# Regrouping query weights as they land, moving FFN weight loads behind a transpose, and a new front order in a linear-attention block kernel

## Chip, cores and metric

The kernel runs on one core of a Trainium2 chip. The metric is the device time of one execution in microseconds; the median of the runs is compared.

## What is computed

The input x has 2048 tokens of 640 features. Block A is attention with 32 heads of 20 features over four segments of 512 tokens, with a running memory between the segments; block B is a feed-forward block with 1728 hidden features. Both add to the residual. All tensors are bf16.

```python
q, k, v = heads(ln(x) @ wq), heads(ln(x) @ wk), heads(ln(x) @ wv)      # 32 heads, 4 segments of 512
for s in range(4):
    p = softmax(qs @ ks.T * scale + causal_mask)
    a_dot = p @ vs
    a_mem = (phi(qs) @ M) / (phi(qs) @ z + 1e-6)
    outs.append(g * a_mem + (1 - g) * a_dot)
    M, z = M + phi(ks).T @ vs, z + sum(phi(ks))
h = x + concat(outs) @ wo
out = h + silu(ln(h) @ w1) @ w2
```

## The kernel before

The kernel is one straight program for all engines. `build` declares small tasks, each with a name, the engines that may do it, and what it reads and writes. A long string, `ORDER`, gives the sequence of all tasks by hand. Each entry is a task name, then optionally the engine (`/A` ScalarE, `/D` VectorE, `/G` GpSimd, `/S` SyncE) and, after a colon, the slots that its new buffers take (PSUM banks above all). Each engine does its tasks in the order of the list; semaphore waits are derived from reads and writes. A DMA is a task of the engine that issues it, so its place in the list is its place in that engine's queue. The loads of x and of the weights, and all DMA transposes, are issued by SP; the on-chip copies `vt` by SP or ACT. An issuing engine waits at the DMA's place until its inputs are there, and everything behind it on that engine waits too.

The names that matter here, for segment 0 (the first digit) unless said otherwise:

- `x0`, `x1`, `x2`, `x4`, `x8`, `x12`: loads of 128-token blocks (one, one, two, four, four, four). `w_q0`, `w_q1`, `w_q2`: the query weights, chunks 0, 1 to 2 and 3 to 4 of five chunks of 128 rows; `w_k0`, `w_k1` the key weights in two parts. They land raw in `sT` (`wraw`).
- `re_wq0` to `re_wq4`, `re_wk0` to `re_wk4` (the function `rearr`, L692 on ACT, L694 on DVE): a weight's columns regrouped into `wqr` or `wkr`, one task for each of five head groups. Groups 0 to 2 take two operations, groups 3 and 4 three. Each group has 128 columns, four heads of 32 rows: 20 features of one head and 12 (or 8 and 4) borrowed features of a head of the last twelve.
- `n1_st`, `n1_r`, `n1_ap`: statistics, reciprocal root and application of the first layer norm for a token block. `n1_tp` and `n1_te`: transposing by TensorE (L778) and evacuation into `hT` (L790, L791), for blocks 0 to 3. `n1_tr4` and on: the same for the blocks of the next segment by a DMA transpose into `xT` (L798).
- `pr0cwx`, `pr0cwy`: projection of head group c, w = 0 for query and 1 for key, tokens 0 to 255 (x) or 256 to 511 (y) (L866; L871 for `pr010x` and `pr040x`, which work block by block). `qe...`: its evacuation (L882 on ACT, L883 on DVE).
- `vt00` to `vt011` (L914): on-chip copies that collect the borrowed features into three more groups, `QZV`. Those with numbers 0, 3, 6, 9 read groups 0 to 2, the others groups 3 and 4; all of them read the x and the y half.
- `qk0x1`, `qk0x2`, `qk0x3`, `qk4x1`, ... (L964): scores, and `e0x1`, ... their exponentials on ACT (L976), either in two halves (`e0x10`, `e0x12`) or in one (`e0x1+`). `mk...`: the causal mask on GpSimd (L987). The names with 4 use the copied groups. `v00` to `v13` (L827): value projections, and `ve` their evacuation (L842). `av`, `oe`, `tn`, `nm`: probabilities times values and the division. `ex`, `pha`, `phb`, `kt`, `mz`: phi of the keys, its DMA transpose (L1207) and the memory.
- `ot` and `wo` (L1264, L1272): the output's DMA transpose and the output projection. `w_w1_0` to `w_w1_4`: the first FFN weight, one load of 432 KB for each chunk. `h1` (L1307) and `h2` (L1349): the FFN.

The two value projections at the seam of segment 0 and 1 are `v11`, `v12`, `v10`, `v13`, in this order; each reads what `n1_tr5`, `n1_tr6`, `n1_tr4` and `n1_tr7` bring. SP's part of the list in that stretch reads, with the tasks of other engines left out:

```text
vt02 vt011 vt05 vt08 vt04 vt06 vt09 vt01 n1_tr5 kt02 n1_tr6 kt00 w_w1_2 n1_tr4 w_w1_3 w_w1_1 n1_tr7 ot1 ot0 w_w1_4
```

Of the kernel before, what the change touches and what calls it, by code (L numbers as in the profile page):

```python
# [324 lines left out]
D = 640  # L325
# [31 lines left out]
epsg0:0 vpad0 zpad w2z/G:0 fill30:7 warm iota mt mta mtb mm7 x0:0 x1:4 mm0 n1_st1/A:0,0 w_q0:0 w_q1 w_q2 epsc sel  # L357
halfc n1_st0/D:5 n1_r0/G n1_r1/D n1_ap0:0 n1_tp0:4 n1_te0a/A:0 n1_ap1:1 n1_tp1:0 n1_te0b/A n1_te1b/D n1_te1a/A w_k0
re_wq1/D:0 pr010x:4 re_wq4/A re_wq2/D pr020x:2 qe020x/A:0 qe010x/A:0 re_wq3/D re_wq0/D pr000x:5 pr040x:6 w_k1
re_wk2/A:0 qe000x/A:0 re_wk1/D qe040x/A:0 pr011x:0 qe011x/A re_wk0/D pr001x:2 pr021x:5 qe001x/A qe021x/A x2:10,5  # L360
n1_st2/D:3 n1_r2/G qk0x10:0 pr030x:7 w_wv0:0 w_wv1 n1_st3/D:1 n1_r3/G e0x10:4 x4:2,1,11,3 qe030x/A:0 w_wo:0 beta
w_w1_0:0 e0x12 re_wk3/D pr031x:6 n1_ap2:2 re_wk4/D x8/S:6,7,8,9 n1_ap3:0 n1_tp2:0 n1_te2/D n1_st6:4 n1_tp3:4 n1_r6/G
n1_te3/A qe031x/D pr041x:7 qe041x/D qk0x20:0 e0x2+:6 pr030y:4 qe030y/D pr031y:5 qe031y/A pr041y:6 qe041y/A pr040y:7
qe040y/A vt02/S:0 vt011/S vt05/S vt08/S n1_st5:1 qk0x30:0 vt04/S mk0x1_0 mk0x1_256 n1_st4:5 n1_r5/G n1_ap5:1 e0x3+:0
n1_ap6:2 pr000y:4 qe000y/D lsc0 vt07/A pr021y:6 qe021y/D pr001y:5 qe001y/D pr011y:7 ex021:0 qe011y/D pr020y:1 n1_r4/D
mk0x3_0 qe020y/D mk0x3_256 vt010/A pr010y:6 qe010y/D vt00/A vt03/A vt06/S v03:2 ve03/D:0 ex001:1 mk0x3_384 mk0x2_0
v00:4 ve00/D qk0y10:0 e0y12:5 mk0x1_384 pha021:1 pha001:2 v01:6 e0y10 mk0y1_0 mk0x2_256 vt09/S phb021 vt01/S qk4x10:2
phb001 lsc1 n1_st7:7 e4x1+:2 vpad1 v02:0 ve01/D av0x:6 mk4x1_0 n1_ap4:3 n1_r7/G qk4x20:2 e4x2+:1 n1_tr5:0 mk4x1_256
mk4x1_384 ve02/D lsc2 lsc3 oe0x/D:0 mk4x2_0 mk4x2_256 av2x:7 ex041:1 oe2x/D:1 kt02:0 n1_tr6 mk0y1_256 mm2 kt00:1 v11:0
qk4x30:2 e4x30:3 pha011:0 ve11/D:1 tn0x:6 nm0x:3 e4x32 mk4x3_0 pha031:1 qk0ya0:0 mk4x3_256 n1_ap7:2 mk4x3_384 v12:6  # L370
e0ya+:4 w_w1_2 ve12/D av4x:4 oe4x/D:0 mz00:5 ma00/A:2,5 qk1ya0:0 e1ya2:0 tn2x:6 nm2x:0 av6x:7 oe6x/D:1 e1ya0 tn4x:6
nm4x:1 qk2ya0:2 kvz e2ya2:1 tn6x:7 mm3 nm6x:2 n1_tr4 v10:0 n1_st11:2 e2ya0 qk0y20:4 e0y2+:6 w_w1_3 w_w1_1 mk0y2_0
kg00/G:0 mk0y2_256 n1_tr7 v13:2 n1_r11/G qk3ya0:4 e3ya0:3 ve10/D n1_st9:6 n1_r9/D pha041:2 ex031:2 mm6 ve13/D ot1:0
wo1:0 n1_st8:3 e3ya2 ot0 ex011:0 wo0:2 rs1 n2_st1:0 mk0y1_384 w_w1_4 phb011 qk4ya0:4 e4ya0:2 n2_r1/D kg02/G e4ya2 rs0
n2_ap1:0 n2_st0:0 pr101:0 qe101/A:0 av0y:1 qk0y30:2 e0y3+:0 w_w2_0/S pr120:6 zf0 n2_r0/D oe0y/D:0 pr100:7 mk0y3_0
ex101:0 qk5ya0:2 n2_ap0:3 e5ya2:4 n2_tr1:0 phb041 qe100/D e5ya0 qe120/D:0 pr121:0 qe121/D qk4y10:4 mk0y3_256 tn0y:1
# [36 lines left out]
h2_2_2 e19b2 h2_2_3 mk18a_0 n2_r5/G qk19a0:0 h2_3_0:4 h2_3_1 e19a2:0 o2 ad17:0 vp22/S e19a0 n2_ap5:3 n2_tr5 out2/S
mk19a_0 vp24/S ex200:0 kh14/D av18:6 oe18/D:0 vt210/A phb200 qk20b0:0 e20b+:3 h2_3_2 mk19b_0 h2_3_3 o3 vp25/S ex201:1
# [48 lines left out]
def build(nc, es, A_x, A_wq, A_wk, A_wv, A_wo, A_beta, B_x, B_w1, B_w2, out):  # L463
# [209 lines left out]
    def rearr(k, wi, dst, prio):  # L673
# [3 lines left out]
        for c in range(5):  # L677
# [10 lines left out]
            def emit(eng, ops=ops, rr=rr, ww=ww):  # L688
                fns = []
                for o, i_ in ops:  # L690
                    if eng == AC:
                        fns.append(lambda e, o=o, i_=i_: e.activation(out=o, in_=i_, func=ACT.Identity))  # L692
                    else:
                        fns.append(lambda e, o=o, i_=i_: e.tensor_copy(out=o, in_=i_))  # L694
# [730 lines left out]
```

## Time and profile before

| | |
|---|---|
| median of 3 runs | 298.89 us (298.69 to 299.05) |
| profiled execution | 298.33 us |
| its span in the trace | 296.6 us |
| TensorE, ScalarE, VectorE, GpSimd busy | 285.0, 217.5, 222.8, 139.9 us |
| granted TensorE clock | 1.00 |

The span is what the profiler recorded from the first to the last instruction; the device time of the same execution is 1.7 us longer. Busy times are sums of the durations of instructions. Matmuls are pipelined, so a busy TensorE is not one at its peak.

### The profile page before, as it was taken

Reading aid. Unit: us, or ns where it says so; the run is one execution under the profiler, and the core shown is the slowest. Engines: PE = TensorE matmul, PEld = TensorE weight load, DVE = VectorE, ACT = ScalarE, POOL = GpSimd, SP = SyncE. Lnnn points to the kernel's source line nnn. Section 1 sums busy time; section 2 is a strip of 40 time slices with the busy share of each in tenths; the row PEclk is TensorE's granted clock in tenths of the full one; section 3 lists DMA queues with packets and bytes.
Section 4 is the critical chain, followed back from the end, with each engine's and each line's share of the span. In section 5 each row is a group of like instructions: output and inputs, shape, how many; then the busy total and the mean of one; then the engine's idle time right before and its main releaser. Section 6 shows DMA issues by size and latency. Waiting matters only on the chain.

```text
span 296.6 us, 7437 instructions
## 1 busy us (share of the span) xinstructions
PE 285.0 (96%) x2991; PEld 167.6 (56%) x2991; DVE 222.8 (75%) x506; ACT 217.5 (73%) x266; POOL 139.9 (47%) x257
## 2 busy tenths in 40 slices
PE   7897879999999999999999999999999999999997
PEld 5775445545665455566643444465665457764575
DVE  3897889768989789899678967759967688626522
ACT  5875979999999899999879999788759751014400
POOL 6246834744656477646525656355576620200000
PEclk9999999999999999999999999999999999999999
DMA  7968772804943321254462400154181023220002
GB/s 208 366 209 114 192 105 68 221 18 98 168 89 75 74 39 26 37 111 66 97 140 51 77 1 2 26 75 88 20 102 32 0 59 76 68 67 25 22 22 91
DMA packets 49906, 25.40 MB, mean 86 GB/s; under 512 B 39488, under 2 KB 48032, under 8 KB 49872
## 3 DMA queue, kind: packets, MB, share of 16 engines
q1 hardware_dynamic: 48204, 23.18, 37.3%
q10 hardware_dynamic: 1668, 1.74, 1.9%
q8 instruction: 24, 0.39, 0.6%
q14 instruction: 10, 0.08, 0.1%
HBM read 10.41 MB, written 2.62 MB: 44 GB/s over the span
## 4 chain that ended last, share of the span: by engine, by line
PE 76%; DVE 8%; DMA 7%; ACT 4%; POOL 2%; issue 2%; SPq 1%; DVEq 0%; ACTq 0%
PE ps_all L1349 19%; PE ps_all L1307 15%; PE ps_all L866 12%; PE ps_all L1272 7%; PE ps_all L964 7%; PE ps_all L827 5%; PE ps_all L1008 5%; ACT PT L976 3%; DMA x_tok<-in_A_x_dram 3%; DMA xT<-xn_rot 2%; PE ps_all L1038 1%; DMA w_sb<-w_sb 1%; PE ps_all L1092 1%; PE ps_all L1225 1%; POOL PT L987 1%
## 5 line engine op out<-in xcount | busy, mean ns | idle before, releaser
L976 ACT ACTIVATE PT<-ps_all 128x1024 bf16<-128x1024 f32 (+1 forms) x120 | 153.1, 1310 | 17.7 <-PE ps_all L964 16.5
L987 POOL TENSOR_SCALAR_AFFINE_SELECT PT<-PT 128x512 bf16<-128x512 bf16 x128 | 81.5, 647 | 59.1 <-ACT PT L976 57.0
L1349 PE MATMUL ps_all<-w_sb,sT 128*128 128x320 bf16 (+2 forms) x462 | 64.9, 295 | 0.0
L1307 PE MATMUL ps_all<-hT,w_sb 128*128 128x512 bf16 (+1 forms) x325 | 63.0, 337 | 0.5 <-DVE sT L1322 0.4
L1316 ACT ACTIVATE th<-ps_all 128x512 f32<-128x512 f32 (+2 forms) x70 | 34.0, 505 | 35.1 <-PE ps_all L1307 31.0
L1349 PEld LDWEIGHTS ps_all<-w_sb,sT 128*128 128x128 bf16 x462 | 43.2, 98 | 18.3 <-issue 1.8
L1322 DVE SCALAR_TENSOR_TENSOR sT<-th,ps_all 128x512 bf16<-128x512 f32 (+2 forms) x70 | 37.8, 561 | 17.1 <-ACT th L1316 16.1
L1307 PEld LDWEIGHTS ps_all<-hT,w_sb 128*128 128x128 bf16 x325 | 29.8, 98 | 25.9 <-issue 3.2
L763 POOL TENSOR_TENSOR rst<-rst,eps_c 128x1 f32<-128x1 f32 x32 | 18.4, 579 | 25.1 <-DVE rst L757 23.5
L742 DVE BATCH_NORM_STATS2 stt<-x_tok 128x6 f32<-128x320 bf16 x62 | 27.2, 481 | 1.8 <-DMA x_tok<-in_A_x_dram 1.4
L1362 DVE SCALAR_TENSOR_TENSOR x_tok<-ps_all,x_tok 128x640 bf16<-128x640 f32 (+3 forms) x18 | 13.3, 745 | 16.7 <-PE ps_all L1349 16.6
L1070 POOL TENSOR_TENSOR otok<-on 128x320 bf16<-128x320 bf16 x24 | 19.0, 796 | 11.5 <-DVE on L1062 11.5
L1272 PE MATMUL ps_all<-wo_sb,oT 128*128 128x320 bf16 x160 | 23.8, 299 | 0.0
L883 DVE CAST QK<-ps_all 128x512 bf16<-128x512 f32 x23 | 15.7, 688 | 8.8 <-PE ps_all L866 8.7
L1062 DVE TENSOR_TENSOR on<-ps_all,rd 128x640 bf16<-128x640 f32 x24 | 19.8, 825 | 0.9
L827 PE MATMUL ps_all<-wv_sb,xT 128*128 128x320 bf16 x120 | 18.3, 299 | 1.6 <-DMA xT<-xn_rot 1.3
L1272 PEld LDWEIGHTS ps_all<-wo_sb,oT 128*128 128x128 bf16 x160 | 15.0, 98 | 7.2 <-issue 1.8
L866 PE MATMUL ps_all<-xT,wkr 128*128 128x512 bf16 x75 | 18.7, 380 | 0.0
L866 PE MATMUL ps_all<-xT,wqr 128*128 128x512 bf16 x75 | 18.2, 380 | 0.0
L842 DVE CAST Vx<-ps_all 128x640 bf16<-128x640 f32 x15 | 12.3, 819 | 5.9 <-PE ps_all L827 5.8
L1008 PE MATMUL ps_all<-PT,Vx 128*32 128x512 bf16 (+3 forms) x384 | 16.4, 301 | 0.1
L769 DVE TENSOR_SCALAR xn_rot<-x_tok,mvt,rst 128x640 bf16<-128x640 bf16 x32 | 14.8, 473 | 1.7 <-POOL rst L763 1.0
(106 smaller groups left out, 338.3 us busy)
## 6 DMA issues: line engine op xcount, KB each, us to landing
w_sb<-in_B_w_dram SPq DMA_DIRECT2D x5, 432.0 KB, 6.1
x_tok<-in_A_x_dram SPq DMA_DIRECT2D x3, 640.0 KB, 8.4
w_sb<-in_B_w_dram SPq DMA_DIRECT2D x3, 480.0 KB, 4.4
out_dram<-x_tok ACTq DMA_DIRECT2D x8, 160.0 KB, 1.8
out_dram<-x_tok SPq DMA_DIRECT2D x7, 160.0 KB, 2.0
QKV<-QK SPq DMA_DIRECT2D x12, 72.0 KB
wo_sb<-in_A_wo_dram SPq DMA_DIRECT2D x1, 800.0 KB, 10.0
sT<-in_A_wq_dram SPq DMA_DIRECT2D x2, 320.0 KB, 4.3
```

The costliest lines, as they stand in the source:

```text
L742: T.add(DV, lambda e, hh=hh: e.bn_stats(out=stt[:, s, 6 * hh:6 * hh + 6], in_=xb[:, 320 * hh:320 * hh + 320]), reads=R((xa, xsub)), writes ...
L827: fns.append(lambda e, c=c, hh=hh: e.matmul(bank(ps, hh)[:, 0:320], lhsT=xT_[:, c, 128 * i:128 * i + 128], rhs=wv_sb[:, c, 320 * hh:320 * ...
L866: fns = [lambda e, kc=kc: e.matmul(bank(ps)[:, lo:hi], lhsT=wt[:, kc, c, :], rhs=xT_[:, kc, lo:hi], start=(kc == 0), stop=(kc == NC - 1)) ...
L964: fns.append(lambda e, j=j, o=o, r=r, q0=q0, q1=q1, qa=qa, ka=ka: e.matmul(ps_all[:, o:o + q1 - q0], lhsT=ka[32 * r:32 * r + DH, 128 * j:1 ...
L976: T.add(AC, lambda e: e.activation(out=pt[:, pta.slot, q0:q0 + nq, 0:width], in_=sc3[:, b0:b0 + nq, 0:width], func=ACT.Exp, scale=SCALE), ...
L987: T.add(PO, lambda e: e.affine_select(out=v, in_=v, pattern=[[0, 4], [1, 128]], compare_op=ALU.is_ge, fill=0.0, base=0, channel_multiplier ...
L1008: fns.append(lambda e, j=j, r=r, h=h, pa=pa, pt=pt, co=co, q0=q0, ji=ji: e.matmul(bank(po)[32 * r:32 * r + 32, q0:hi], lhsT=Vx[:, vx.slot, ...
L1272: fns.append(lambda e, c=c, hh=hh: e.matmul(bank(ps, hh)[:, 0:320], lhsT=oT[:, c, 128 * i:128 * i + 128], rhs=wo_sb[:, c, 320 * hh:320 * h ...
L1307: fns = [lambda e, c=c: e.matmul(bank(ps)[:, lo:hi], lhsT=w1_sb[:, c, 128 * f:128 * f + 128], rhs=hT[:, c, lo:hi], start=(c == 0), stop=(c ...
L1316: T.add(AC, lambda e: e.activation(out=th[:, tha.slot, lo:hi], in_=bank(ps)[:, lo:hi], func=ACT.Tanh, scale=0.5), reads=R((ps, [0])), writ ...
L1322: T.add(DV, lambda e: e.scalar_tensor_tensor(out=sT[:, f, lo:hi], in0=th[:, tha.slot, lo:hi], scalar=1.0, in1=bank(ps)[:, lo:hi], op0=ALU. ...
L1349: fns.append(lambda e, f=f, t0=t0, fr=fr, hh=hh, n=n: e.matmul(bank(pa, hh)[:, 0:n], lhsT=sT[:, f, t0:t0 + 128], rhs=w2_sb[:, fr, c0 + 320 ...
```

## The change

In `rearr`, the query groups 1 and 2 become two tasks each: `re_wq1` and `re_wq2` regroup chunks 0 to 2 and wait for `w_q0` and `w_q1` only; `re_wq1b` and `re_wq2b` regroup chunks 3 and 4 and wait for `w_q2`. The other groups stay as they were.

```diff
-            rr, ww = [(sT0, ["k0", "k1"] if wi else ["q0", "q1", "q2"])], [(W[k], [c])]
+            ww = [(W[k], [c])]
+            pieces = [("", 0, 3, ["q0", "q1"]), ("b", 3, 5, ["q2"])] if wi == 0 and c in (1, 2) else \
+                [("", 0, 5, ["k0", "k1"] if wi else ["q0", "q1", "q2"])]
...
-                for o, i_ in ops:
+                for o, i_ in [(o[:, k0:k1], i_[:, k0:k1]) for o, i_ in ops]:
...
-            G.task(f"re_{k}{c}", {DV: 0.36 if c < 3 else 0.42, AC: 0.72}, emit, rr, ww, prio + c)
+            for tg, k0, k1, sub in pieces:
+                rr = [(sT0, sub)]
+                G.task(f"re_{k}{c}{tg}", {DV: 0.36 if c < 3 else 0.42, AC: 0.72},
+                       lambda eng, emit=emit, rr=rr, k0=k0, k1=k1: emit(eng, rr=rr, k0=k0, k1=k1), rr, ww, prio + c)
```

The list is redone up to `v02`, and three loads are moved behind that point. The front of the new list:

```text
x0:3 x1:6 mm0 n1_st1/A:0,0 w_q0:0 halfc sel n1_st0/D:3 epsc w_q1 n1_r0/D re_wq2/A:0 w_q2 w_k0 n1_ap0:2 n1_tp0:0
n1_te0a/A:0 n1_r1/D n1_ap1:0 n1_tp1:2 n1_te1a/A re_wq1/D re_wq4/D n1_te0b/A n1_te1b/A re_wq2b/D pr040x:1 qe040x/A:0
w_k1 re_wk0/A:0 x2:0,1 w_wv0:0 re_wq1b/D pr010x:2 qe010x/A:0 re_wq3/D re_wq0/D pr000x:4 re_wk1/D w_wv1 pr011x:6
qe000x/A:0 qe011x/A x4:9,2,10,5 pr001x:5 qe001x/A re_wk2/D pr021x:7 qe021x/A:0 n1_st2/D:1 w_wo:0 n1_st3/D:4 qk0x10:0
e0x10:3 pr030x:4 qe030x/A:0 pr020x:6 qe020x/A e0x12 n1_r2/G n1_ap2:0 n1_tp2:0 re_wk3/D pr031x:4 beta re_wk4/D n1_r3/G
n1_ap3:1 n1_tp3:5 n1_te3/A n1_te2/D pr041x:7 qe041x/D qk0x20:0 e0x22:0 pr041y:6 n1_st4:2 qe031x/D pr030y:5 qe030y/D
x8/S:7,8,4,11 n1_r4/D e0x20 mk0x2_0 pr031y:7 qe041y/D pr040y:2 pr010y:0 qk0x30:3 qe031y/A qe040y/D pr001y:1 mk0x1_0
mk0x2_256 pr020y:2 pr000y:7 mk0x1_256 mk0x1_384 vt07/A:0 vt011/S vt01/S vt02/S vt010/S vt08/A e0x3+:4 vt04/S n1_st5:0
qe010y/D qe001y/D pha001:1 qe000y/D n1_r5/D qe020y/D pr011y:1 qe011y/D n1_ap5:3 pr021y:0 qe021y/A v03:6 mk0x3_0
n1_st7:0 mk0x3_256 mk0x3_384 n1_r7/G pha021:2 vt06/A n1_st6:6 vt09/S qk0y10:2 vt00/S vt05/S ve03/D:0 n1_r6/G v00:0
n1_tr5:0 ex001:0 phb001 kt00:0 vt03/A lsc0 e0y1+:5 mk0y1_0 n1_ap4:1 n1_tr4 ex021:2 n1_ap6:0 n1_tr6 mk0y1_256 ve00/D
phb021 kt02:1 lsc1 vpad1 v01:6 ve01/D w_w1_0:0 qk4x10:2 e4x12:2 e4x10 mk4x1_0 v02:0
```

In the list before, the same stretch is:

```text
x0:0 x1:4 mm0 n1_st1/A:0,0 w_q0:0 w_q1 w_q2 epsc sel halfc n1_st0/D:5 n1_r0/G n1_r1/D n1_ap0:0 n1_tp0:4 n1_te0a/A:0
n1_ap1:1 n1_tp1:0 n1_te0b/A n1_te1b/D n1_te1a/A w_k0 re_wq1/D:0 pr010x:4 re_wq4/A re_wq2/D pr020x:2 qe020x/A:0
qe010x/A:0 re_wq3/D re_wq0/D pr000x:5 pr040x:6 w_k1 re_wk2/A:0 qe000x/A:0 re_wk1/D qe040x/A:0 pr011x:0 qe011x/A
re_wk0/D pr001x:2 pr021x:5 qe001x/A qe021x/A x2:10,5 n1_st2/D:3 n1_r2/G qk0x10:0 pr030x:7 w_wv0:0 w_wv1 n1_st3/D:1
n1_r3/G e0x10:4 x4:2,1,11,3 qe030x/A:0 w_wo:0 beta w_w1_0:0 e0x12 re_wk3/D pr031x:6 n1_ap2:2 re_wk4/D x8/S:6,7,8,9
n1_ap3:0 n1_tp2:0 n1_te2/D n1_st6:4 n1_tp3:4 n1_r6/G n1_te3/A qe031x/D pr041x:7 qe041x/D qk0x20:0 e0x2+:6 pr030y:4
qe030y/D pr031y:5 qe031y/A pr041y:6 qe041y/A pr040y:7 qe040y/A vt02/S:0 vt011/S vt05/S vt08/S n1_st5:1 qk0x30:0 vt04/S
mk0x1_0 mk0x1_256 n1_st4:5 n1_r5/G n1_ap5:1 e0x3+:0 n1_ap6:2 pr000y:4 qe000y/D lsc0 vt07/A pr021y:6 qe021y/D pr001y:5
qe001y/D pr011y:7 ex021:0 qe011y/D pr020y:1 n1_r4/D mk0x3_0 qe020y/D mk0x3_256 vt010/A pr010y:6 qe010y/D vt00/A vt03/A
vt06/S v03:2 ve03/D:0 ex001:1 mk0x3_384 mk0x2_0 v00:4 ve00/D qk0y10:0 e0y12:5 mk0x1_384 pha021:1 pha001:2 v01:6 e0y10
mk0y1_0 mk0x2_256 vt09/S phb021 vt01/S qk4x10:2 phb001 lsc1 n1_st7:7 e4x1+:2 vpad1 v02:0
```

Behind `v02` the sequence of compute tasks is unchanged, except that `n1_ap4` has gone ahead. `n1_tr5`, `kt00`, `n1_tr4`, `n1_tr6`, `kt02` have gone ahead, in this order. `w_w1_1` and `w_w1_3` now follow `n1_tr7`, and `w_w2_0` stands one place earlier. SP's stretch becomes:

```text
vt011 vt01 vt02 vt010 vt04 vt09 vt00 vt05 n1_tr5 kt00 n1_tr4 n1_tr6 kt02 w_w1_0 w_w1_2 n1_tr7 w_w1_1 w_w1_3 ot1 ot0 w_w1_4
```

More of the change, by code (lines that the diff above doesn't have):

```diff
@@ L356 @@
 ORDER = """
[L357 to L376, printed above, removed]
```

183 lines of the change are left out of this document (102 added, 81 removed).

## The prediction

> **What bounds the kernel now.** I read the page first, then busy time by stretch, then the waits of TensorE, then the timelines of PE, ACT and SP around the two largest waits. The first two lines below are of the page (busy time; the chain that ended last), the rest is busy time by stretch: PE, PEld, DVE, ACT, POOL with their counts, then clock, DMA share and GB/s.
>
> ```profile
> PE 285.0 (96%) x2991; PEld 167.6 (56%) x2991; DVE 222.8 (75%) x506; ACT 217.5 (73%) x266; POOL 139.9 (47%) x257
> PE 76%; DVE 8%; DMA 7%; ACT 4%; POOL 2%; issue 2%; SPq 1%; DVEq 0%; ACTq 0%
> 8.30:12.23 3.93, 3.93 (x45) 3.46 (x45) 3.42 (x16) 3.44 (x12) 0.54 (x2) 1.00 1.07 372
> 12.23:21.54 9.31, 9.27 (x108) 7.29 (x108) 8.89 (x31) 8.41 (x12) 3.92 (x10) 1.00 0.79 266
> 21.54:28.20 6.66, 5.11 (x57) 3.33 (x55) 5.15 (x13) 2.57 (x3) 4.93 (x9) 1.00 0.62 107
> 28.20:44.20 16.00, 13.18 (x198) 7.59 (x197) 13.28 (x31) 13.93 (x12) 9.88 (x20) 1.00 0.87 145
> 44.20:60.00 15.80, 15.50 (x199) 8.93 (x196) 13.81 (x34) 15.34 (x18) 9.99 (x19) 1.00 0.58 145
> ```
>
> TensorE is the bound of the whole (285.0 of 296.6 us). The list is changed almost only ahead of 50 us, so what counts is idle TensorE there. From 8.30 to 21.54 there is none (3.93 + 9.27 = 13.20 busy of 13.24). From 21.54 to 28.20 it idles 1.55 us, from 28.20 to 44.20 2.82 us, and in the second of these ACT is busier than PE (13.93 of 16.00). The waits of PE, for 0 to 44 us (three rows) and for 44 us to the end (the last row, its longest): us, times, longest.
>
> ```profile
> PE ps_all L964 <- DMA w_sb<-w_sb: 1.6, 1, 1.6
> PE ps_all L827 <- DMA xT<-xn_rot: 1.3, 1, 1.3
> PE ps_all L964 <- DVE otok L1137: 0.9, 1, 0.9
> PE ps_all L1307 <- DVE sT L1322: 0.4, 1, 0.4
> ```
>
> Three waits are worth a look: scores (L964) for the on-chip copies "vt", the value projection v13 (L827) for the transpose n1_tr7, and scores behind a division on DVE. After 44 us no wait is over 0.4 us, so a shift won there should reach the end one to one.
>
> **The change part by part.** First the clearest: w_w1_1 and w_w1_3 go behind n1_tr7. Timelines of SP, PE and ACT (start, length), and two rows of DMA issues (KB where known, us from issue to landing).
>
> ```profile
> 33.02 1.05 SPq L581 DMA_DIRECT2D w_sb<-in_B_w_dram  x2
> w_sb<-in_B_w_dram SPq DMA_DIRECT2D x2, 432.0 KB, 6.3
> 35.03 1.21 SPq L798 DMA_TRANSPOSE xT<-xn_rot  x1
> xT<-xn_rot SPq DMA_TRANSPOSE x1, 7.4
> 42.45 1.53 PE L827 MATMUL ps_all<-wv_sb,xT 128*128 128x320 bf16 x10 [1.31 <-DMA xT<-xn_rot]
> 43.91 0.40 PE L964 MATMUL ps_all<-w_sb 20*128 20x256 bf16 x8
> 44.24 2.89 PE L1272 MATMUL ps_all<-wo_sb,oT 128*128 128x320 bf16 x20
> 41.18 1.88 ACT L976 ACTIVATE PT<-ps_all 128x2048 bf16<-128x2048 f32 x1 [0.21 <-PE ps_all L964]
> 44.36 1.02 ACT L976 ACTIVATE PT<-ps_all 128x1024 bf16<-128x1024 f32 x1 [1.30 <-PE ps_all L964]
> ```
>
> The two loads go out at 33.02, the transpose at 35.03 lands 7.4 us later (42.4), and v13 stands still for 1.31 us. In the new list w_w1_0 and w_w1_2 precede n1_tr7 instead, but they follow five transposes that end near 31 (below), so they go out about 2 us ahead of the old pair. With the 6.3 us of the old pair they land by 37.7 (the second goes out at 31.4) and n1_tr7, 2.5 us after them as in the trace (42.4 against 33.6 + 6.3 = 39.9), by about 40.2. PE comes to v13 at 42.45 - 1.31 = 41.14. The stall goes. What is late next is ACT: qk3ya0 (43.91) takes PSUM slots 4 to 7, which e0y2+ reads until 41.18 + 1.88 = 43.06. So qk3ya0 starts at about 43.13 and its exponential, 0.45 us behind it as now (43.91 to 44.36), at 43.58: 44.36 - 43.58 = 0.78 us won, not 1.31. Above it is bounded by ACT's whole gap, 1.30; below by 0.
>
> Next, the front. wq groups 1 and 2 are regrouped in chunks 0 to 2 and chunks 3 and 4. Rows: an issue and its landing, ACT and PE timelines, and regrouping copies by shape (busy, mean ns).
>
> ```profile
> 2.21 0.43 SPq L581 DMA_DIRECT2D sT<-in_A_wq_dram  x1
> sT<-in_A_wq_dram SPq DMA_DIRECT2D x1, 320.0 KB, 4.1
> 6.51 0.91 ACT L790 ACTIVATE hT<-ps_all 128x384 bf16<-128x384 f32 x2 [1.11 <-PE ps_all L778]
> 8.30 0.72 PE L871 MATMUL ps_all<-hT,wqr 128*128 128x128 bf16 x10 [0.94 <-DVE wqr L694]
> L694 DVE COPY wqr<-sT 128x400 bf16<-128x400 bf16 x4 | 1.1, 272 | 0.0
> L694 DVE COPY wkr<-sT 128x80 bf16<-128x80 bf16 x2 | 0.4, 190 | 0.0
> L692 ACT ACTIVATE wkr<-sT 128x240 bf16<-128x240 bf16 x1 | 0.4, 404 | 0.0
> ```
>
> The second load (chunks 1 and 2) lands at 2.21 + 4.1 = 6.31, while ACT waits until 6.51 anyway. re_wq2 now runs there first: two operations, of 240 and 144 elements, 404 ns and somewhat less, ending near 6.9, so the first evacuation of hT starts 0.4 us late. ACT then does all four evacuations (one was on DVE), each 0.45 us (0.91 for two) and the last two behind the second transpose: the last ends near 8.6, and the first projection, now pr040x, ends at about 8.9 against 8.85. I take 0.05 us later; the bounds are 0.4 later (the held evacuation in full) and 0.3 earlier (the copies that TensorE waited for until 8.30 are done sooner). On DVE a split group costs four copies where there were two; from 272 ns at 400 elements and 190 at 80 each extra copy is near 0.2 us, so about 0.3 us a group. It costs nothing as long as DVE then waits for the k weights anyway; without that cover it is 0.3 to 0.6 us.
>
> [...]
>
> From 8.30 to 21.54 TensorE does the same 20 half projections, transposes and scores in another order, without a hole to close. So the last projection ends no earlier; 0 won here. In the new list six more evacuations of the y half run on DVE, and layer norm statistics go between them; walking through both engines by the durations above I find no projection waiting for its PSUM slot.
>
> Then the copies vt. Rows: the chain that ended last (start, length), ACT's timeline, and the durations of the copies' issues on ACT (min/median/max in ns).
>
> ```profile
> 21.75 0.44 DVE w_sb L883
> 23.86 3.78 DMA w_sb<-w_sb
> 18.38 1.88 ACT L976 ACTIVATE PT<-ps_all 128x2048 bf16<-128x2048 f32 x1
> 18.49 1.63 ACTq L914 DMA_DIRECT2D w_sb<-w_sb  x1
> 23.99 0.63 ACT L889 ACTIVATE ex<-w_sb 128x512 bf16<-128x512 bf16 x1 [2.64 <-DVE Vx L842]
> 28.22 1.88 ACT L976 ACTIVATE PT<-ps_all 128x2048 bf16<-128x2048 f32 x1 [1.48 <-PE ps_all L964]
> L914 ACTq DMA_DIRECT2D w_sb<-w_sb x4: 701/856/1626, 18.5 to 23.1; - x4
> ```
>
> The last evacuation of the y half ends at 21.75 + 0.44 = 22.19; the copies that read it follow, and the last lands at 23.86 + 3.78 = 27.64, 5.45 us behind it. Only then come qk4x10 and, at 28.22, ACT's long run. In the new list five copies follow the last evacuation as now (three on SP, two on ACT), so the 5.45 us stay. But that evacuation is now qe021y on ACT behind e0x3+, and e0x3+ stands behind vt07 and vt08, which ACT itself issues. Queued behind those two issues on ACT are e0x3+, qe021y, vt06, ex001, vt03 and the exponentials of qk0y10; v03 waits for e0x3+ as well (slot 6), and the copies for qe021y. vt07 can go at about 18.48, when its inputs are ready, as now. With 0.8 us an issue (the median is 0.86) e0x3+ runs from 20.1 to 22.0 and qe021y ends at about 22.3: 0.1 us later than 22.19. The issue of 1.63 us I read as one that had a small activation (lsc0) queued ahead of it behind a 1.88 us exponential; in the new list nothing of that kind precedes vt07. Bounds: 0.05 earlier (0.70 each; then TensorE is later than ACT) and 1.8 later (1.63 each).
>
> The exponentials of qk4x10 come in two halves: 2 x 1.02 less the overlap in place of 1.88, so 0.06 us more. ACT's run from 28.22 to 43.06 is otherwise the same work in the same order, and the third wait of PE (0.9 us) lies inside it, where ACT is the later of the two. w_w1_0 leaving the first flood of loads lets x8 land sooner, which nobody waits for: 0.
>
> Sum: -0.78 + 0.10 + 0.06 = -0.62 us (the 0.05 of the start is contained in the 0.10, since the later of two arrivals counts). The profiled execution took 298.33 us (span 296.6) and lies 0.56 us under the median of the runs, 298.89; I apply the difference to both: 297.7 for a like execution, 298.3 as the median.
>
> **The rivals.** Rows for them: issues on SP, the projection v12, landings.
>
> ```profile
> 27.28 1.29 SPq L798 DMA_TRANSPOSE xT<-xn_rot  x1
> xT<-xn_rot SPq DMA_TRANSPOSE x1, 4.4
> 34.40 1.53 PE L827 MATMUL ps_all<-wv_sb,xT 128*128 128x320 bf16 x10
> 40.24 2.90 SPq L1264 DMA_TRANSPOSE oT<-otok  x2
> oT<-otok SPq DMA_TRANSPOSE x1, 2.7
> w_sb<-in_B_w_dram SPq DMA_DIRECT2D x1, 432.0 KB, 3.4
> ```
>
> *ACT's issues hold the chain.* If vt07 costs 1.63 us and vt08 0.86, e0x3+ ends at 18.48 + 2.49 + 1.88 = 22.85, qe021y near 23.2, and the long run starts 1.0 us late: -0.78 + 1.0 + 0.06 = +0.3, so 299.2. For it speaks the 1.63 row and ex001 at 23.99, which stood behind two such issues; against it that three of four issues took under 0.9. At 1.8 us late it is slower by 1.1.
>
> *The wait moves to ot1.* w_w1_1 and w_w1_3 now go out near 36.3 and 36.8, ahead of the transpose ot1 at 40.24. With 6.3 us they land by 43.1; ot1, now landing at 40.24 + 2.7 = 42.9, could follow as n1_tr7 did, and the output projection, due at 43.5, waits 0.1 to 2.1 us. I price it at 0.4: 298.7. Against it: the pair has three microseconds more of a head start than n1_tr7 gave it, and a load with no other load beside it landed in 3.4 us. [...]
>
> *Slower: the transposes in front of v12.* n1_tr6 goes out at 27.28 now. In the new order SP does n1_tr5, kt00, n1_tr4 first, and kt00 waits for phb001 on DVE, behind st7, st6 and ve03. From 24.7 and 1.25 us each, n1_tr6 goes out at 28.45 and with 4.4 us lands at 32.9; v12 starts at 34.40, so 1.5 us are spare. If phb001 comes late or the landing takes n1_tr7's 7.4 us (35.85), v12 is 1.45 us late, and with it mz00, qk1ya0 and ACT's run, which has no slack: -0.62 + 1.45 = +0.8, so 299.7. It decides from a delay of 2.1 us in SP's line (the spare 1.5 and the 0.62 won). For it: five transposes in a row, never seen here; against: the spare time.
>
> *Nothing arrives.* The stall at v13 is hidden by ACT altogether, 298.9.
>
> **How the numbers follow.** A measurement of this kernel can tell about 0.2% (0.6 us) from no change. Forecast: 0.58, of which 0.44 lies beyond 0.6 us (the start gaining, or all of ACT's gap closing) and 0.14 inside. ACT's issues: 0.14, of which 0.04 slower. ot1: 0.10, of which 0.01 slower. v12: 0.15, slower. Nothing: 0.03. Faster 0.44; same 0.14 + 0.10 + 0.09 + 0.03 = 0.36; slower 0.04 + 0.01 + 0.15 = 0.20. The forecast's own range is 297.6 (all of ACT's 1.30 us won) to 298.8. For 8 in 10 the range has to take in v12's case: 297.6 to 299.7.
>
> **What would show it.** Right: PE no longer waits for xT at v13; qk3ya0 follows the end of e0y2+ within 0.1 us, and ACT's idle time before the exponential of qk3ya0 falls from 1.30 to about 0.5; ACT's long run starts between 28.1 and 28.5; TensorE is full from the first projection to 21.6. Wrong: the exponential of 1.88 us that was at 18.38 starts after 20.5 (issues on ACT); PE waits for xT near 34 (v12) or for oT near 43 (ot1); the first projection starts after 8.7 (evacuations behind re_wq2), or a hole between 9 and 21 us. If the time falls by over 1.3 us, something shortened ACT's run or the copies' 5.45 us, which I hold constant.

## The result and the profile after

The changed kernel takes 299.1 us in the median (298.47 to 300.25) where the kernel before takes 298.08 us on the same chip: a ratio of 1.0037, interval 1.0025 to 1.0049, so 1.1 us slower. The forecast was 298.3 us, 0.6 us faster. The profiled execution of the changed kernel took 300.03 us (span 298.3); against that of before (298.33, span 296.6) it is 1.7 us longer, of which some 0.7 us is particular to these two executions (300.03 lies 0.9 us over its median, 298.33 lies 0.25 us over 298.08).

Line numbers behind `rearr` are six higher than before. Busy time and chain of the page:

```profile
PE 282.3 (95%) x2968; PEld 167.2 (56%) x2991; DVE 222.8 (75%) x513; ACT 217.1 (73%) x266; POOL 139.8 (47%) x255
PE 76%; DVE 9%; DMA 6%; ACT 3%; issue 2%; SPq 1%; POOL 1%; ACTq 1%; DVEq 0%
```

Busy time by stretch (PE, PEld, DVE, ACT, POOL with their counts), in the stretches shown of before:

```profile
8.30:12.23 3.93, 2.74 (x35) 2.32 (x33) 1.74 (x8) 1.99 (x7) 0.00 (x0) 1.00 1.05 370
12.23:21.54 9.31, 9.29 (x111) 7.19 (x110) 8.61 (x29) 6.21 (x11) 4.61 (x9) 1.00 0.66 217
21.54:28.20 6.66, 5.52 (x52) 3.75 (x50) 6.06 (x18) 5.12 (x6) 4.75 (x10) 1.00 0.41 66
28.20:44.20 16.00, 12.72 (x200) 7.39 (x198) 11.87 (x27) 12.81 (x14) 8.96 (x16) 1.00 0.70 176
44.20:60.00 15.80, 14.65 (x187) 8.12 (x192) 13.83 (x35) 15.03 (x18) 9.34 (x19) 1.00 0.62 152
```

TensorE does the same work (a few matmul records are missing) and is full from 12.23 to 21.54, but it now has a hole of 1.19 us between 8.30 and 12.23, and it idles 3.28 us from 28.20 to 44.20 (2.82 before) and 1.15 us from there to 60 (0.30 before). The four largest waits between its fillers (the dummy matmuls at the start) and 46 us (us, times, longest):

```profile
PE ps_all L970 <- DMA w_sb<-w_sb: 1.7, 1, 1.7
PE ps_all L872 <- DVE wkr L697: 1.2, 1, 1.2
PE ps_all L833 <- ACT PT L982: 1.1, 1, 1.1
PE ps_all L970 <- DVE otok L1143: 0.9, 1, 0.9
```

ACT's timeline at the places that the prediction spoke of:

```profile
21.89 1.88 ACT L982 ACTIVATE PT<-ps_all 128x2048 bf16<-128x2048 f32 x1 [2.94 <-PE ps_all L872]
30.66 1.94 ACT L982 ACTIVATE PT<-ps_all 128x1024 bf16<-128x1024 f32 x2 [2.28 <-PE ps_all L970]
46.06 1.02 ACT L982 ACTIVATE PT<-ps_all 128x1024 bf16<-128x1024 f32 x1 [0.50 <-PE ps_all L970]
```

The wait of v13 for its transpose is gone, and ACT's gap ahead of the exponential of qk3ya0 is 0.50 us where it was 1.30. But the long exponential e0x3+ starts at 21.89 where it started at 18.38, TensorE waits 1.1 us for it (v03), and ACT's long run starts at 30.66 where it started at 28.22. The chain that ended last (start, length; some rows left out) names what stands in between:

```profile
3.70 6.89 DMA sT<-in_A_wk_dram
10.68 0.43 DVE wkr L697 x2
...
19.51 1.63 ACTq L920
21.17 0.67 ACTq L920
21.89 0.93 ACT PT L982
...
23.66 0.39 ACT w_sb L888
24.06 0.81 SPq L920
24.92 0.79 SPq L920
25.75 4.33 DMA w_sb<-w_sb
```

vt07 (1.63 us) and vt08 (0.67 us) are issued by ACT, then comes e0x3+, then the last evacuation (qe021y), then three more copies on SP, the last of which lands at 30.08 (27.64 before). The k weights at the top landed at 10.59, 6.89 us after their issue; in most of the other traces that took 6.0 to 6.3 us.

### The profile page after: what moved, and what is told of

It reads as the page before. It is cut to its first block, busy times and chain, and to the rows that moved or that the text cites. A ratio compares the mean times of both kernels' runs of the same rounds, so it can differ in the third digit from the quotient of the medians.

```text
span 298.3 us, 7419 instructions
## 1 busy us (share of the span) xinstructions
PE 282.3 (95%) x2968; PEld 167.2 (56%) x2991; DVE 222.8 (75%) x513; ACT 217.1 (73%) x266; POOL 139.8 (47%) x255
## 4 chain that ended last, share of the span: by engine, by line
PE 76%; DVE 9%; DMA 6%; ACT 3%; issue 2%; SPq 1%; POOL 1%; ACTq 1%; DVEq 0%
PE ps_all L1355 19%; PE ps_all L1313 15%; PE ps_all L872 12%; PE ps_all L970 7%; PE ps_all L1278 6%; PE ps_all L833 5%; PE ps_all L1014 5%; DMA sT<-in_A_wk_dram 2%; ACT PT L982 2%; DMA x_tok<-in_A_x_dram 2%; DVE stt L748 2%; PE ps_all L1098 2%; DMA w_sb<-w_sb 1%; PE ps_all L1044 1%; PE ps_all L1231 1%
## 5 line engine op out<-in xcount | busy, mean ns | idle before, releaser
L1313 PE MATMUL ps_all<-hT,w_sb 128*128 128x512 bf16 (+1 forms) x315 | 61.1, 336 | 2.0 <-DVE sT L1328 0.7
L872 PE MATMUL ps_all<-xT,wkr 128*128 128x512 bf16 x67 | 16.9, 380 | 1.1 <-issue 0.8
L872 PE MATMUL ps_all<-xT,wqr 128*128 128x512 bf16 x70 | 17.3, 380 | 0.4 <-issue 0.2
L775 DVE TENSOR_SCALAR xn_rot<-x_tok,mvt,rst 128x640 bf16<-128x640 bf16 x32 | 14.2, 453 | 2.7 <-POOL rst L769 2.4
```

The costliest lines, as they stand in the source:

```text
L872: fns = [lambda e, kc=kc: e.matmul(bank(ps)[:, lo:hi], lhsT=wt[:, kc, c, :], rhs=xT_[:, kc, lo:hi], start=(kc == 0), stop=(kc == NC - 1)) ...
L1313: fns = [lambda e, c=c: e.matmul(bank(ps)[:, lo:hi], lhsT=w1_sb[:, c, 128 * f:128 * f + 128], rhs=hT[:, c, lo:hi], start=(c == 0), stop=(c ...
```

## The experiments

Two theories to begin with: vt07 and vt08 ahead of e0x3+ on ACT (the rival "ACT's issues hold the chain"), or the new order on VectorE, which meets the key weights without cover. Two starting points tell them apart: the changed kernel with one thing undone, and the kernel before with one thing done. To compare executions that do not start alike, I use two distances in each trace: A from TensorE's first projection to the start of ACT's long run (before: 28.22 - 8.30 = 19.92), and B from there to the exponential of qk3ya0 (before: 44.36 - 28.22 = 16.14). In the change the first projection starts 0.17 us earlier, A is 2.61 us longer and B 0.74 us shorter: together 1.70 us, the whole difference of the two profiled executions. All ratios are to the kernel before.

| kernel | ratio (interval) | A, us | B, us |
|---|---|---|---|
| before | 1 | 19.92 | 16.14 |
| the change | 1.0037 (1.0025 to 1.0049) | 22.53 | 15.40 |
| e1: change, vt07 and vt08 behind e0x3+ | 1.0001 (0.9981 to 1.0021) | 20.13 | 15.39 |
| e2: before, FFN loads behind n1_tr7 | 0.9988 (0.9968 to 1.0007) | 19.86 | 15.35 |
| e3: change, k weights covered | 1.0033 (1.0017 to 1.0049) | 21.60 | 15.40 |
| e4: before, vt07 ahead of e0x3+ | 1.0043 (1.0026 to 1.0061) | 21.50 | 15.75 |
| e5: change, early load on ACT | 1.0059 (1.0041 to 1.0076) | 21.11 | 15.40 |
| e6: before, split regrouping | 0.9992 (0.9978 to 1.0006) | 19.95 | 15.34 |
| e7: e2 and vt01 on ACT | 0.9995 (0.9978 to 1.0011) | 19.34 | 15.34 |
| e8: change, FFN loads at the old place | 1.0041 (1.0018 to 1.0064) | 22.02 | 15.49 |
| e9: change, vt011 first on ACT | 1.0025 (1.0006 to 1.0044) | 21.42 | 15.40 |
| e10: e7, vt010 first on ACT | 1.0132 (1.0097 to 1.0166) | 22.32 | 16.63 |
| e11: e1, vt010 on ACT, ve03 earlier | 1.0025 (1.0003 to 1.0046) | 20.22 | 15.41 |
| e12: change, early copy on ACT | 1.0016 (0.9998 to 1.0034) | 20.65 | 15.40 |

**e1: the two issues behind the exponential.**

```diff
-mk0x1_384 vt07/A:0 vt011/S vt01/S vt02/S vt010/S vt08/A e0x3+:4 vt04/S
+mk0x1_384 vt011/S:0 vt01/S vt02/S vt010/S e0x3+:4 vt07/A vt08/A vt04/S
```

> The changed kernel with vt07 and vt08 placed behind e0x3+ in ACT's order, all else as changed. Theory 1 (the two issues on ACT hold e0x3+, and with it v03, qe021y and the last copies): the issues run under the 1.88 us exponential, e0x3+ starts near 19.5 instead of 21.9, qe021y ends near 22.5 instead of 24.0, ACT's long run starts near 29.0 instead of 30.7, and the time falls by 1.5 to 1.8 us against the changed kernel, to about 297.5 (0.2% under the kernel before). Rival K (the k weights' late landing and the 1.2 us hole of TensorE at 10 us are the loss): the copies are not what ends last, the time falls by less than 0.5 us, to 298.6 or more. Rival N (an issue takes ACT's time wherever it stands): no change, 299.1.

The ratio fell from 1.0037 to 1.0001, by about 1.1 us where I expected 1.5 to 1.8. ACT's timeline:

```profile
19.12 1.88 ACT L982 ACTIVATE PT<-ps_all 128x2048 bf16<-128x2048 f32 x1 [0.95 <-PE ps_all L970]
19.18 1.32 ACTq L920 DMA_DIRECT2D w_sb<-w_sb  x1
28.66 1.94 ACT L982 ACTIVATE PT<-ps_all 128x1024 bf16<-128x1024 f32 x2 [2.04 <-PE ps_all L970]
```

The issue now runs under the exponential and holds nobody; A is 20.13, close to before.

**e2: the FFN loads alone**, in the list before.

```diff
-e0y2+:6 w_w1_3 w_w1_1 mk0y2_0 kg00/G:0 mk0y2_256 n1_tr7 v13:2
+e0y2+:6 mk0y2_0 kg00/G:0 mk0y2_256 n1_tr7 w_w1_1 w_w1_3 v13:2
```

> The kernel before with only w_w1_1 and w_w1_3 moved behind n1_tr7. If the step that I priced at 0.78 us holds, PE's wait for xT at v13 (1.31 us) is gone, ACT's idle time ahead of the exponential of qk3ya0 falls from 1.30 to about 0.5, and the time falls by 0.7 to 0.8 us, to about 297.3. Rival (ACT hides it, or the wait moves to ot1): no change, 298.1.

The wait for xT is gone, and ACT's gap is 0.50:

```profile
44.16 1.02 ACT L976 ACTIVATE PT<-ps_all 128x1024 bf16<-128x1024 f32 x1 [0.50 <-PE ps_all L964]
```

B is 0.79 us shorter than in the trace of before, as predicted. The time is only 0.12% (0.4 us) lower, and its interval includes no gain. e8 below bears on why.

**e3: cover for the k weights.** The projection of the queries of head group 2 and its evacuation go back ahead of what needs the key weights, as in the list before.

```diff
-pr000x:4 re_wk1/D w_wv1 pr011x:6 qe000x/A:0 qe011x/A
+pr000x:4 pr020x:3 re_wk1/D w_wv1 pr011x:6 qe000x/A:0 qe020x/A:0 qe011x/A
...
-pr030x:4 qe030x/A:0 pr020x:6 qe020x/A e0x12
+pr030x:4 qe030x/A:0 e0x12
```

> The changed kernel with the projection pr020x and its evacuation moved back ahead of the first key projection, so that TensorE has one more query projection (0.55 us) to do while the key weights land. Rival K: the hole before pr011x shrinks from 1.2 to about 0.65 us and the time falls by about 0.5 us, to 298.6. Theory 1: the wait of e0x3+ for ACT's issues follows the last evacuation of groups 3 and 4, which comes no earlier by more than the hole shrinks, so at most the same 0.5 us; if the key weights land at 9.5 us as in the profile before, there is no hole and no change, 299.1.

The hole is gone and with it 0.9 us of A, but the time is that of the change (1.0033), and v03 waits 1.1 us for e0x3+ as there. ACT's timeline, and TensorE's wait:

```profile
20.28 0.67 ACTq L920 DMA_DIRECT2D w_sb<-w_sb  x1
20.99 1.88 ACT L982 ACTIVATE PT<-ps_all 128x2048 bf16<-128x2048 f32 x1 [2.86 <-PE ps_all L872]
```

```profile
PE ps_all L833 <- ACT PT L982: 1.1, 1, 1.1
```

The k weights are not the main cause. The 0.9 us of A fit the 0.9 us by which the profiled execution of the change lies over its median.

**e4: vt07 ahead of e0x3+, in the list before.** No other task moves.

```diff
-e0x3+:0 n1_ap6:2 pr000y:4 qe000y/D lsc0 vt07/A pr021y:6
+vt07/A e0x3+:0 n1_ap6:2 pr000y:4 qe000y/D lsc0 pr021y:6
```

> The kernel before with vt07 alone placed ahead of e0x3+ on ACT (it stood behind it and behind lsc0). If the 1.63 us of that issue come from lsc0 queued ahead of it, as I read it, the issue now takes 0.7 to 0.9 us and e0x3+ starts near 19.3. If the first copy issued on ACT takes 1.63 us wherever it stands, e0x3+ starts near 20.1. The end: v03 then waits for e0x3+ (slots 2 and 3) until about 22.0, and ex021 and the issues behind it come up to 0.6 us later; the time rises by 0 to 0.6 us, to 298.1 to 298.7.

```profile
18.90 1.62 ACTq L914 DMA_DIRECT2D w_sb<-w_sb  x1
20.57 1.88 ACT L976 ACTIVATE PT<-ps_all 128x2048 bf16<-128x2048 f32 x1 [1.69 <-PE ps_all L866]
```

One issue ahead of the long exponential gives 1.0043, as much as the whole loss and twice what I expected at most (0.6 us); TensorE waits 1.5 us for that exponential. The issue takes 1.62 us though lsc0 is no longer ahead of it, so my reading of the 1.63 us row (lsc0 ahead of vt07) falls.

**What makes that issue slow.** Each later copy on ACT takes 0.64 to 0.86 us. e5 asks whether it is the first DMA of ACT that is slow.

```diff
-x1:6 mm0 n1_st1/A:0,0 ... re_wk0/A:0 x2:0,1 w_wv0:0
+x1:6 mm0 x2/A:0,1 n1_st1/A:0,0 ... re_wk0/A:0 w_wv0:0
```

> The changed kernel, with one early load (x2, tokens 256 to 511 of x) issued by ScalarE ahead of its first statistics, near 2.1 us, in place of SP near 4.2 us. Nothing else is changed, so vt07 is no longer the first DMA that ScalarE issues. Theory F (the first DMA that ScalarE issues costs about 1.6 us wherever it stands, each later one 0.7 to 0.9): the issue of x2 takes about 1.6 us, that of vt07 0.7 to 0.85, the long exponential e0x3+ starts 0.8 us earlier than with the change (near 21.1, if the first projection starts near 8.1), and the time falls by 0.6 to 0.9 us, to 298.2 to 298.5. Rival G (vt07's own shape or place makes it cost 1.6 us): vt07 still takes 1.6 us and the time stays at 299.1. A third outcome would be a first projection that starts later because x2 lands among the query weights: then the time rises by as much as the first projection is late.

```profile
1.11 0.48 ACTq L579 DMA_DIRECT2D x_tok<-in_A_x_dram  x1
19.43 1.62 ACTq L920 DMA_DIRECT2D w_sb<-w_sb  x1
```

The early load took 0.48 us and vt07 1.62 as before: the theory falls. (The time rose: x1 landed at 4.95 in place of 3.57, beside x2, and the first projection started at 9.42.) Three theories were left: ACT's first copy between on-chip tiles, a start together with SP's, or vt07 itself. e9 exchanges vt07 and vt011; e10 makes vt010 the first, two microseconds behind SP's start.

```diff
-vt07/A:0 vt011/S vt01/S vt02/S vt010/S vt08/A e0x3+:4
+vt011/A:0 vt07/S vt01/S vt02/S vt010/S vt08/A e0x3+:4
```

> The changed kernel, with vt07 and vt011 exchanged: ScalarE issues vt011 first (ahead of vt08 and the long exponential), SP begins with vt07. An early load issued by ScalarE did not shorten vt07's issue, so it is not the queue's first DMA that is slow. Theory C (the first on-chip copy that ScalarE issues is slow, whichever it is): vt011 takes 1.5 to 1.6 us, vt07 on SP 0.8, and the time stays at 298.8 to 299.3. Theory S (the issue is slow because SP begins its copies at the same moment): the same here. Theory O (vt07's own addresses make it slow): vt011 takes 0.7 to 0.85 us on ScalarE, vt07 shows 1.5 us or so on SP, the long exponential starts 0.8 us earlier and the time falls to 298.2 to 298.6.

```diff
-lsc0 vt07/A pr021y:6 ... mk0x3_256 vt010/A vt01/A pr010y:6
+lsc0 pr021y:6 ... mk0x3_256 vt010/A vt07/A vt01/A pr010y:6
```

> The kernel of e7 (list before, w_w1_1 and w_w1_3 behind n1_tr7, vt01 on ScalarE), with vt07 moved behind vt010 on ScalarE. vt010 is then ScalarE's first copy; it goes out two microseconds after SP has begun its copies. Theory C (the first on-chip copy that ScalarE issues is slow): vt010 takes 1.5 us or so, vt07 0.7; the three copies behind them end 1.5 us later than in e7, and the time is 0.4 to 1.0 us above e7. Theory S (slow because SP begins at the same moment): vt010 and vt07 take 0.65 to 0.75 us each, the copies behind them end 0.7 us later, and the time is 0.2 to 0.7 us above e7. Theory O (vt07 itself): vt010 0.7, vt07 1.5, and the time as by C.

ACT's issues in e9, and then in e10:

```profile
18.86 1.26 ACTq L920 DMA_DIRECT2D w_sb<-w_sb  x1
20.15 0.65 ACTq L920 DMA_DIRECT2D w_sb<-w_sb  x1
```

```profile
21.20 1.47 ACTq L914 DMA_DIRECT2D w_sb<-w_sb  x1
22.70 0.70 ACTq L914 DMA_DIRECT2D w_sb<-w_sb  x1
```

Whichever copy ACT issues first is slow (1.26 and 1.47 us), and vt07 as the second takes 0.70: the first copy it is. e9's ratio of 1.0025 does not differ from the change's within the intervals. e10 lost 1.3%, far more than the 0.4 to 1.0 us I expected: ACT's five issues end at 25.83 where e7's end at 23.93, and the last of them landed 5.22 us after its issue, so that TensorE waited 3.8 us for copies. That landings grow like this I had not foreseen. Part of the loss has another cause: behind the wait of 3.8 us the granted clock of TensorE was 0.53 from 30.4 to 34.0, and a value projection on the chain that ended last took 2.78 us there (at 31.06), where the next three on it took 1.46 to 1.52. That is why B is 16.63, 1.3 us longer than e7's; all six executions of e10 have a mean clock below 1.00 (0.994 in four, 0.989 in two).

e12 is the counter-test: a small copy of zeros added early on ACT, where it waits for x (`lsc1` on GpSimd is made to read its target).

```diff
-fill30:7 warm iota
+fill30:7 warm wcp/A iota
...
+    dma("wcp", [(C, ["zpad"])], [(C, ["wcp"])], lambda e: e.dma_start(out=wcp[0:8, :], in_=zpad[0:8, :]), ...)
```

> The changed kernel, with one small on-chip copy added (8 partitions of 256 zeros into a tile of its own) that ScalarE issues near 2.3 us, ahead of its first statistics, where it waits for x anyway. The copies so far: whichever one ScalarE issues first took 1.26 to 1.63 us, those behind it 0.65 to 0.85, and an early load from HBM (0.48 us) did not change that. Theory (it is the first copy between on-chip tiles on ScalarE that is slow): the added copy takes 1.2 to 1.6 us, vt07 then takes 0.65 to 0.85, the long exponential starts 0.5 to 0.9 us earlier against the first projection than in the changed kernel, and the time falls by 0.4 to 0.8 us, to 298.3 to 298.7. Rival (the cost lies in the place or the size of the borrowed-feature copies, not in their being first): the added copy takes under 1 us, vt07 1.3 to 1.6 us as before, and the time stays at 298.8 to 299.3.

```profile
1.10 1.25 ACTq L603 DMA_DIRECT2D wcp<-zpad  x1
18.94 0.75 ACTq L923 DMA_DIRECT2D w_sb<-w_sb  x1
20.46 1.88 ACT L985 ACTIVATE PT<-ps_all 128x2048 bf16<-128x2048 f32 x1 [2.09 <-PE ps_all L875]
```

The added copy takes the 1.25 us, vt07 then 0.75, and the ratio falls to 1.0016, about 0.6 us under the change (the intervals overlap). A is 20.65, 0.95 us under e3's. What is left above e1 is 0.5 us of A, and the two issues ahead of the exponential are not what it waits for: the chain that ended last in e12 runs, as in e1, through SP's eight issues in a row. Against the first projection they begin 0.19 us later (TensorE waited 0.2 us for the key weights), take 0.07 us longer, and the last copy lands in 4.06 us where e1's took 3.79.

**e6: the split alone**, in the list before.

```diff
-re_wq1/D:0 pr010x:4 re_wq4/A re_wq2/D pr020x:2
+re_wq1/D:0 re_wq1b/D pr010x:4 re_wq4/A re_wq2/D re_wq2b/D pr020x:2
```

> The kernel before, with the regrouping of query groups 1 and 2 cut in two parts each, the second part directly behind the first on VectorE; the list is otherwise the old one. Theory (the split does not carry the loss): VectorE does four small copies more, some 0.2 us each; the first projection starts 0 to 0.3 us later and the time rises by 0 to 0.3 us, to 298.3 to 298.6. Rival (the split itself costs what was lost): the first projection starts 0.6 us or more later and the time is 299.0 or more.

The time is 0.9992 of before, the interval from 0.9978 to 1.0006: no cost to be seen in it. Its trace says why that proves little in this list: the first projection starts at 9.35, 1.05 us late (x1 landed 0.7 us later than in the trace of before, and the wait for the query groups is 1.27 us where it was 0.94), A is the same, and B is 0.80 us shorter, since v13's wait falls to 0.33 us and ACT's 0.50 us gap covers it. A front that is late by up to 0.8 us can hide in that stall.

**e8: the FFN loads at the old place**, in the changed kernel.

```diff
-e0y2+:6 mk0y2_0 kg00/G:0 mk0y2_256 n1_tr7 w_w1_1 w_w1_3 v13:2
+e0y2+:6 w_w1_3 w_w1_1 mk0y2_0 kg00/G:0 mk0y2_256 n1_tr7 v13:2
```

> The changed kernel, with w_w1_3 and w_w1_1 back at their old place, ahead of n1_tr7. Theory (the move of the two loads wins its 0.7 to 0.8 us in the new order too): TensorE waits for xT at v13 again, 0.8 to 1.4 us, the gap of ScalarE ahead of the exponential of qk3ya0 grows from 0.5 to about 1.3 us, and the time rises to 299.7 to 300.0. Rival (the loss of the front took the place of that stall, since everything up to v13 comes later by the same amount and the transposes do not): no wait for xT, and the time stays at 299.1.

ACT's row for the exponential of qk3ya0 in the three other kernels whose FFN loads stand at the old place: e8, e4 and e6. The number in brackets is the gap ahead of it; in the trace of before it was 1.30.

```profile
45.83 1.02 ACT L982 ACTIVATE PT<-ps_all 128x1024 bf16<-128x1024 f32 x1 [0.60 <-PE ps_all L970]
```

```profile
45.96 1.02 ACT L976 ACTIVATE PT<-ps_all 128x1024 bf16<-128x1024 f32 x1 [0.91 <-PE ps_all L964]
```

```profile
44.64 1.02 ACT L981 ACTIVATE PT<-ps_all 128x1024 bf16<-128x1024 f32 x1 [0.50 <-PE ps_all L969]
```

The gap is 0.50 wherever the loads are moved, and at the old place 1.30, 0.91, 0.60 and 0.50. So by these traces the move wins 0 to 0.8 us, 0.33 in the mean of the four, and the trace that I had read held the largest of them. They are one trace each of four kernels, and in the other three ACT's long run starts 1.1 to 2.1 us later than before, so they don't show how much one kernel varies. A later front is one reason for a smaller stall; it is not the only one, since the smallest (e6) isn't the one that comes latest. e8's own time (1.0041) does not differ from the change's.

**e7 and e11: two tries at a better kernel.** e7 is e2 with the last of SP's copies on ACT; e11 is e1 with one more copy there.

```diff
-mk0x3_256 vt010/A pr010y:6 ... vt09/S phb021 vt01/S qk4x10:2
+mk0x3_256 vt010/A vt01/A pr010y:6 ... vt09/S phb021 qk4x10:2
```

> The kernel before, with w_w1_1 and w_w1_3 behind n1_tr7 (the part of the change that was tried alone) and one copy more moved: vt01, the last of eight on SP, goes to ScalarE between vt010 and vt00, where ScalarE's queue waits for nothing but the evacuations. Theory (the last on-chip copy sets the start of ScalarE's long run; each issue on SP is 0.8 us): the last copy is issued 0.8 us earlier on SP and lands 0.8 us earlier, the exponential of qk4x10 starts 0.4 to 0.8 us earlier, and the time is 296.9 to 297.3, 1.0 to 1.4 us under the kernel before. Rival (ScalarE's own queue becomes the later one: vt01 there pushes vt00, vt03 and the exponential behind them by 0.8 us): the last copy lands no earlier, and the time is 297.5 to 298.5.

```diff
-vt02/S vt010/S e0x3+:4 vt07/A vt08/A vt04/S ... vt06/A n1_st6:6 ... vt05/S ve03/D:0
+vt02/S e0x3+:4 vt07/A vt08/A vt010/A vt04/S ... vt06/A ve03/D:0 n1_st6:6 ... vt05/S
```

> The kernel of e1 (the change with vt07 and vt08 behind the long exponential), with vt010 too issued by ScalarE under that exponential in place of SP, and ve03 ahead of the statistics of block 6 on VectorE. In e1 SP's eight issues ran without a pause from 18.75 to 25.05 and TensorE waited 0.85 us for ve03. Theory (issues on SP and ve03 are what is left of the loss): SP ends its copies 0.7 us earlier, the wait for ve03 falls under 0.2 us, ScalarE's long run starts 0.25 to 0.6 us earlier than in e1, measured from the first projection (20.13 there), and the time is 297.8 to 298.1. Rival (ScalarE's own last copy, vt03, is then the last): the long run starts as in e1 and the time is 298.3.

e7's trace shows the gain: long run at 27.62, A 0.58 us shorter than before, B 0.80, and its execution took 297.18 us. The times do not: 0.9995, interval 0.9978 to 1.0011. The profiled execution is the fastest of the twelve; why the others fall short of it stays open. In e11 the long run starts as the rival had it (A is 20.22, in e1 20.13), but not for its reason: the last copy is still SP's. Three of SP's copies have to wait for the last evacuation, whatever stands ahead of them; the last of the three goes out 15.34 us after the first projection, 0.41 us sooner than in e1, but takes 4.29 us to land (3.79 in e1), so the gain is lost again. The wait for ve03 is gone, without use. Its ratio of 1.0025 lies above e1's 1.0001; their intervals overlap and the traces agree in A and B. Five of its twelve executions have a mean granted clock of 0.994 and took 299.20 to 300.31 us; the seven at 1.00 have a median of 298.43, and e1 had none below 1.00. So most of the difference goes with the clock, not with A or B. No version is shown to beat the kernel before; e2 and e7 come nearest.

## Why the prediction was wrong

*The step that failed* is the +0.10 for the copies on ACT ("with 0.8 us an issue ... in the new list nothing of that kind precedes vt07"). The pair took 1.63 + 0.67 = 2.30 us, and the row of 1.63 us that I quoted was already the right price: vt07 was ACT's first copy before, under the cover of a 1.88 us exponential, and is the first in the new list, without it. I explained an outlier away by a story (lsc0) that one trace could not test. e3, without the late k weights, gives the term its size. There vt07 goes out 0.36 us later against the first projection than before, the pair takes 2.24 us in place of 1.6, and the last evacuation ends 15.00 us after the first projection, where it was 13.89: +1.11 for the +0.10. The prediction's own sign for it, a long exponential that starts after 20.5, came (21.89).

*The 5.45 us from the last evacuation to the last landing*, held constant, became 6.02 in e3 and 6.03 in the change: another 0.57. The issues behind the evacuation took the same time; the last copy took 4.32 and 4.33 us to land where it took 3.78. With the 1.11 that makes the 1.68 us by which A grew in e3, and e1, with the pair behind the exponential, takes back 1.47 of them. What makes a landing longer is not shown.

The rival "ACT's issues hold the chain" named the mechanism and had 0.14. It counted one long issue and one median, 2.49 us, which is close to the 2.30 measured, but put the long run only 1.0 us late. It left out the later start of vt07 and the longer landing.

*The 0.78 us at v13* came as worked out in the traces (B falls by 0.74 in the change, by 0.79 in e2), with ACT's 0.50 us gap as the next limit. The time of e2 shows about half of it, and its interval includes none; e8 shows that the stall is smaller in other traces. In the change's own traces A without the late k weights (+1.68, e3) and B (-0.74) add up to +0.9 us; by the ratios the change lost 1.1 and e3 1.0.

*The start* was 0.05 us later by the prediction; the first projection started at 8.13 (8.30 before), with fillers ahead of it of the same length. *The full TensorE from the first projection to 21.6* did not hold: in that execution the k weights left a hole of 1.19 us, which I had covered by an assumption. In the other traces with this front it is 0 to 0.7 us, and e3, which has none, is no faster. *The split* cost nothing in the trace of the change: VectorE ends its copies at 8.57 and then waits 2.11 us for the key weights, and the first projection waits for ACT's evacuation, not for VectorE. (In e1's trace it does wait for VectorE, 1.30 us, behind query weights that land at 7.57, and starts at 8.53.) In the trace of the change VectorE's copies of 128x96 take 182 ns and those of 128x400 take 277 (means): a quarter of the elements at two thirds of the time, and the wait for the key weights hid what that costs.

*The rivals at ot1 and v12* did not come: in the change TensorE waits for neither transpose. *The range* held the 299.1 by luck: it was laid around 298.89, the median of three runs, and the same kernel took 298.08 in the median of 22. As a difference the range was -1.3 to +0.8 us, and the 1.1 measured lies outside it. The sign was wrong, and the chance of slower (0.20) too small, since it hung on v12 and gave the issues 0.04.

## What to carry to other kernels

An issue on ACT held the activation behind it here: in the change 1.63 and 0.67 us of issues stand directly ahead of e0x3+ on the chain. Price such an issue by its own row, in front of whatever long activation it delays, and put it directly behind that activation, where it held nobody here (e1: 1.32 us of issue under 1.88 us of e0x3+). Do not set the longest of four issues aside without a reason that a run has tested; ask first what is special about its place. And a stall behind a transfer that is read from one execution need not be of that size in the next: three other kernels with the loads at the old place showed 0 to 0.4 us where the first trace showed 0.8. State a range as a difference to the kernel before, so that it doesn't hang on the median of three runs.

## What the runs showed of the hardware

The first copy between on-chip tiles that ScalarE issued took 1.25 to 1.63 us, whichever copy it was (vt07, vt011, vt010, or 4 KB of zeros at 1.10 us), and every later one 0.64 to 0.86; a load from HBM ahead of it (0.48 us) did not take its place. What is done in that time no trace shows. SP's first copy took 0.82 to 0.91 us. In the change the first issue, 1.63 us, was not small beside the 4.33 us that the last copy took to land, and it stood on the chain that ended last.

The thirty identical filler matmuls at the start took 4.89 us in the profiled execution of before and 6.33 in that of e2, whose list is the same up to 30 us. In slices of 1 us from 2.12 on TensorE has 7, 7, 11 and 11 matmuls in before, but 7, 7, 6, 7 and 7 in e2: the rate rises at about 4.1 us in before and not by 7.1 us in e2. The profile gives a granted clock of 1.00 for all these slices, so it doesn't name the cause. PE's timelines:

```profile
1.12 4.89 PE L619 MATMUL ps_all<-zpad 128*128 128x256 bf16 x30 [1.12 <-DVE zpad L596]
```

```profile
1.13 6.33 PE L619 MATMUL ps_all<-zpad 128*128 128x256 bf16 x30 [1.13 <-DVE zpad L596]
```

The first projection followed between 8.13 and 8.95 us in 12 of the 14 traces. Part of the scatter of single times, some 2 us between the fastest and the slowest of a kernel, may come from there; it is why distances inside a trace separated the kernels better than the times did.

Another part goes with the granted clock. In e10 the clock was about half for 3.4 us, right behind a wait of 3.8 us, and that stretch alone makes a mean of 0.994 over the 299.7 us (an estimate: 3.4 us at half rate). Waits of up to 2.1 us in the other traces (e11) left it at 1.00. Of the 99 executions of the kernel before that were timed beside e1 to e12, eight show a mean of 0.994, and they took 299.16 to 300.25 us; the other 91 have means of 297.95 to 298.28 in their four sets. Whether those eight had such a wait no kept trace shows.
